# Second MLP of an attention-and-two-MLPs kernel: splits for the output product placed earlier, row tiles stored within it, last pass in halves

## The chip, the cores and the metric

The kernel runs on one core of one Trainium2 chip. The metric is the time of one execution on the device in microseconds (us); the kernel before takes 1617.16 us (median of three runs, 1616.46 to 1618.07). PE is the matrix engine, PEld its weight loads, DVE the vector engine, ACT the scalar engine, POOL the third elementwise engine, SP the engine that issues nearly all DMAs of this part.

## What is computed

A packed attention, a first MLP and a second MLP. Only the second MLP is touched:

```python
def _moe2_ref(x, w_in, w_out):          # x: 4608 x 512, w_in: 512 x 2048, w_out: 2048 x 512
    h = x @ w_in
    relu6 = np.clip(h + 3.0, 0.0, 6.0)
    g = h * relu6 / 6.0
    return (g @ w_out).astype(np.float32)
```

## The kernel before

Class `Second` computes the second MLP, transposed, so that tokens lie along the free dimension. It runs six passes ("pairs", n = 0 to 5) of 768 tokens, each two groups of N = 384. In each pair `hidden(n)` makes `x @ w_in` and the activation, and `project(n)` makes the output product. Both products are cut in 2 x 2 blocks and computed by seven block products instead of eight (numbers k = 1 to 7, with sums of blocks before and after). Each fp32 operand is split in a high part (an ACT cast, `split_hi`, L1136) and a low part (a DVE subtraction, `split_lo`, L1141), and each block product is three matmuls: high weights by high and by low data, low weights by high data (L1097 to L1099 in `hidden`, L1181 to L1183 in `project`). All matmuls are 128 x 384.

`hidden` has 56 steps (f, k): f = 0 to 7, seven products for each, 6 matmuls a step, in the order of `order_h`: the products of f overlap those of f + 1. After a step, `after(f, k)` queues the sums that read its PSUM bank: `h1` (ACT copy, then DVE L1067), `hu` (DVE L1058, later L1070) and `hv` (DVE L1061, L1062). A later product accumulates into a bank that such a sum still has to read, so PE waits for the sum. For each of the four blocks of f, ACT then computes a Relu (L1042) and DVE the gate (L1045), which writes the tile `g`. `soon(steps, fn)` delays a piece of work by some steps. For each odd f the two columns f - 1 and f of a g tile are complete; then `t1` (DVE L1116) and the two halves of the split of the first operand follow. These splits feed steps s = 0 to 3 of `project`, so four of them are made in `hidden`, one for each pair of f.

`project` has 28 steps, seven products (order 1, 5, 6, 3, 7, 2, 4) of four steps, 12 matmuls a step. Step s also queues the sums of step s + 4 and the split of step s + 3. There are four split buffers (`ro`). Step 0 of `project` is issued before the last two steps of `hidden`. The seven products end in the tiles `o1`, `ou`, `ov` and `oc`, each two blocks of 128 output columns for 384 tokens. `ou` is complete after step 15 and `ov` after step 19 and one add on POOL (L1169); these two hold the second 384 tokens of the pair. `oc` is complete after step 23 and `o1` after step 27, for the first 384.

`store` turns a 128-token tile back with four PE transposes into a PSUM bank, multiplies by 1/6 on ACT into `st` (three buffers) and issues one DMA of 128 rows, or, for tokens of the ninth and last block, two of 64 rows, on SP. The six stores of a pair wait in the list `out`; `hidden` of the next pair takes one every seven steps. The stores of the last pair run after its last product.

Weights come from DRAM in tiles `ws` of 512 KB (two DMAs, L962), six buffers, on SP: after each `project` step, and after every second `hidden` step, the next tile is requested into the buffer just used, so a tile is requested six tiles ahead. SP, ACT and DVE work strictly in the order in which the program issues.

Of the kernel before, what the change touches and what calls it, by code (L numbers as in the profile page):

```python
# [18 lines left out]
def tile_pack_attention_two_mlps(ctx: ExitStack, tc, q, k, v, p, w_in1, w_out1, w_in2, w_out2, out):  # L19
# [8 lines left out]
    nc = tc.nc  # L28
    B, H, S, D = q.shape
# [3 lines left out]
    P = 128  # L33
    T = 512
    NI = T // P
    TAIL = S - T
# [3 lines left out]
    KC = DM // P  # L40
# [26 lines left out]
    ident = const.tile([P, P], F32, name="ident")  # L67
# [16 lines left out]
    early, busy, other = [True], [True], [False]  # L84
# [571 lines left out]
    for j in range(2, B - 1):  # L656
        c, d = QPB * (j + 2), QPB * (j + 1)
# [266 lines left out]
    N = 384  # L924
    NPAIR = NBLK * T // (2 * N)
    ROW = {1: 0, 2: 1, 4: 2, 5: 3, 6: 4, 7: 5, 3: 6}
    ORDER_P = (1, 5, 6, 3, 7, 2, 4)
    FD = HF // 2
    WS = 6

    class Second:
# [94 lines left out]
        def hidden(self, n):  # L1026
            X, Y, Z, h1, hu, hv = {}, {}, {}, {}, {}, {}
            later = []

            def soon(steps, fn):  # L1030
                later.append([steps, fn])

            def run_later():
                for item in list(later):
                    item[0] -= 1
                    if item[0] <= 0:
                        later.remove(item)
                        item[1]()

            def act(f, part, h):  # L1040
                r = self.left.tile([P, N], F32, tag="hr", name="hr", bufs=4)
                nc.scalar.activation(out=r, in_=h, func=AF.Relu, bias=three)  # L1042

                def gate():
                    nc.vector.scalar_tensor_tensor(out=self.g[part, f // 2][:, f % 2], in0=r, scalar=6.0, in1=h, op0=ALU.min, op1=ALU.mult)  # L1045

                soon(1, gate)

            def small(tag):
                return self.left.tile([P, N], F32, tag=tag, name=tag, bufs=2)  # L1050

            def after(f, k):
                if k == 1:
                    h1[f] = small("h1")
                    nc.scalar.copy(out=h1[f], in_=X[f])
                elif k == 6:
                    hu[f] = small("hu")
                    nc.vector.tensor_add(out=hu[f], in0=h1[f], in1=Y[f])  # L1058
                elif k == 7:
                    hv[f] = small("hv")  # L1060
                    nc.vector.tensor_add(out=hv[f], in0=h1[f], in1=Y[f])  # L1061
                    nc.vector.tensor_add(out=hv[f], in0=hv[f], in1=Z[f])  # L1062
                    act(f, (1, 1), hv[f])
                elif k == 2:
                    act(f, (0, 0), X[f])
                elif k == 4:
                    nc.vector.tensor_add(out=h1[f], in0=h1[f], in1=Y[f])  # L1067
                    act(f, (1, 0), h1[f])
                elif k == 3:
                    nc.vector.tensor_add(out=hu[f], in0=hu[f], in1=Z[f])  # L1070
                    act(f, (0, 1), hu[f])
                    if f % 2:
                        soon(2, lambda: self.t1(f // 2))
                        soon(3, lambda: self.split_hi(f // 2))
                        soon(5, lambda: self.split_lo(f // 2))

            for fd in range(FD):
                for part in ((0, 0), (0, 1), (1, 0), (1, 1)):
                    self.g[part, fd] = self.left.tile([P, 2, N], F32, tag=f"g{part[0]}{part[1]}{fd}", name=f"g{part[0]}{part[1]}{fd}")
            seq = self.order_h()  # L1080
            xs = self.x
            for i, (f, k) in enumerate(seq):
                if i == len(seq) - 2:
                    next(self.projected)
                if i % 2 == 0:
                    w = self.weights()
                if k == 1:
                    X[f] = self.bank()[:, 0:N]
                elif k == 6:
                    Y[f] = self.bank()[:, 0:N]  # L1090
                elif k == 5:
                    Z[f] = self.bank()[:, 0:N]
                ps = {1: X, 2: X, 6: Y, 7: Y, 4: Y, 5: Z, 3: Z}[k][f]
                for c in range(2):
                    wh, wl = (w[:, i % 2, a + c * P:a + (c + 1) * P] for a in (0, 2 * P))
                    first, last = k in (1, 6, 5) and c == 0, k in (2, 4, 3) and c == 1
                    mm(ps, lhsT=wh, rhs=xs[k][:, 0, c], start=first, stop=False, skip_group_check=True)  # L1097
                    mm(ps, lhsT=wh, rhs=xs[k][:, 1, c], start=False, stop=False, skip_group_check=True)  # L1098
                    mm(ps, lhsT=wl, rhs=xs[k][:, 0, c], start=False, stop=last, skip_group_check=True)  # L1099
                if i % 2:  # L1100
                    self.load_w()
                run_later()
                after(f, k)
                if i % S7 == 5 and self.out:
                    self.out.pop(0)()
                if i == len(seq) // 2 and self.prep:
                    next(self.prep)
            while later:
                run_later()
            while self.out:  # L1110
                self.out.pop(0)()
# [36 lines left out]
        def project(self, n):  # L1148
            X, Y, Z = [], [], []
            o1, ou, ov, o5, oc = (self.left.tile([P, 2, N], F32, tag=tag, name=tag) for tag in ("o1", "ou", "ov", "o5", "oc"))  # L1150

            def after(k):
                for i in range(2):
# [17 lines left out]
            for s in range(FD * S7):  # L1171
                k, fd = ORDER_P[s // FD], s % FD
                w, ro = self.weights(), self.ro.pop(s)
                acc = {1: X, 2: X, 6: Y, 7: Y, 4: Y, 5: Z, 3: Z}[k]
                if not acc:
                    acc += [self.bank()[:, 0:N] for _ in range(2)]
                for f in range(2):
                    for i in range(2):
                        wh, wl = (w[:, f, a + i * P:a + (i + 1) * P] for a in (0, 2 * P))
                        first, last = k in (1, 6, 5) and fd == f == 0, k in (2, 4, 3) and fd == FD - 1 and f == 1  # L1180
                        mm(acc[i], lhsT=wh, rhs=ro[:, 0, f], start=first, stop=False, skip_group_check=True)  # L1181
                        mm(acc[i], lhsT=wh, rhs=ro[:, 1, f], start=False, stop=False, skip_group_check=True)  # L1182
                        mm(acc[i], lhsT=wl, rhs=ro[:, 0, f], start=False, stop=last, skip_group_check=True)  # L1183
                self.load_w()
                if s % FD == FD - 1:
                    after(k)
                self.sums(s + 4)
                if s + 3 >= FD:
                    self.split(s + 3)
                if self.prep and s and s // FD % 2 == 0:  # L1190
                    next(self.prep, None)
                yield
            if self.prep:
                for _ in self.prep:
                    pass
            for t in range(3):
                self.out.append(lambda t=t: self.store(2 * N * n + N + t * P, (ou, ov), t))
            for t in range(3):
                self.out.append(lambda t=t: self.store(2 * N * n + t * P, (oc, o1), t))

        def store(self, col, halves, t):

            ps = self.bank()
            for e in range(KC):
                nc.tensor.transpose(ps[:, e * P:(e + 1) * P], halves[e // 2][:, e % 2, t * P:(t + 1) * P], ident)
            o = self.left.tile([P, DM], F32, tag="st", name="st", bufs=3)
            nc.scalar.mul(out=o, in_=ps, mul=1.0 / 6.0)
            j, c = divmod(col, T)
            if j < B:
                i = c // P  # L1210
                nc.sync.dma_start(out=out[j * S:j * S + T, :].rearrange("(p i) e -> p i e", i=NI)[:, i, :], in_=o)
            else:
                rows = out.rearrange("(b s) e -> b s e", s=S)[:, T:S]
                for i in range(P // TAIL):
                    nc.sync.dma_start(out=rows[c // TAIL + i], in_=o[i * TAIL:(i + 1) * TAIL])

        def run(self):
            self.left = opened(ctx, "second_l", reuse_waits="tile")
# [168 lines left out]
    for j in range(NBLK):  # L1387
        ws = WINDOWS[j] if j < len(WINDOWS) else []
        order = []
        n = QPB * (j + 1) - 1  # L1390
# [13 lines left out]
        if j in mates:  # L1404
            for g in range(1, NG):
                fs = fuse_steps(j, g)
                lo, hi = [max(0, 18 * g * GF - 24) / (18 * NF) for g in (g - 1, g)]
                for i, fn in enumerate(fs):
                    plan.add(("m", j, g, i), lo + (hi - lo) * 0.7 * (i + 0.5) / len(fs), 6 if len(mates[j]) == 1 else 3, fn, bank=11)
        if j + 1 in mates:  # L1410
            lo = max(at_pp, (18 * 3 * GF - 24) / (18 * NF))
# [86 lines left out]
```

## Time and profile before

| | |
|---|---|
| median of three runs | 1617.16 us |
| span of the profiled execution | 1616.0 us |
| PE busy | 1546.7 us (96%) |
| DVE busy | 1036.1 us (64%) |
| ACT busy | 805.9 us (50%) |
| second MLP, first pair to the end | 876.4 to 1616.0 us |

The span runs from the first to the last instruction of one profiled execution. A busy PE is not PE at its best here: a matmul is shown as 0.34 us long while the next begins 0.17 us after it, so what a wait costs is read from the starts of the matmuls. In the rows further down, a bracket at a row's end is the idle time of the engine before it, and who ended it.

### The profile page before, as it was taken

How to read it: one execution, taken by the hardware profiler on the slowest of the kernel's cores; microseconds unless marked ns; L12 is line 12 of the kernel's file. 1: busy time of each engine (PE TensorE's matmuls, PEld its weight loads, DVE VectorE, ACT ScalarE, POOL GpSimd, SP SyncE). 2: the span in 40 equal slices, each digit the busy share in tenths (PEclk: the TensorE clock that was granted, in tenths of full speed). 3: DMA queues.
4: the chain of work that ended last, by engine and by line, in shares of the span. 5: the costliest groups of instructions: out<-in, count | busy, mean ns of one | idle time of the engine just before them, and what ended most of it. 6: DMA issues, size and time to landing. Idle time of an engine off the chain costs nothing.

```text
span 1616.0 us, 23717 instructions
## 1 busy us (share of the span) xinstructions
PE 1546.7 (96%) x8396; PEld 1333.6 (83%) x8396; DVE 1036.1 (64%) x1765; ACT 805.9 (50%) x1357; POOL 194.4 (12%) x172
## 2 busy tenths in 40 slices
PE   6898998899999999999999999999999999999997
PEld 3576765677777777778888999999999999999997
DVE  5776453765566465653443687687687687687674
ACT  4876544655556546554443353453453453453443
POOL 1432011111121111112231000000000000000000
PEclk9899999999999999999999999999999999999999
DMA  8998785896768776758597878978878988888875
GB/s 213 289 276 271 231 225 122 244 256 178 200 212 223 219 177 204 243 155 245 185 334 230 280 237 255 297 253 257 300 252 255 298 254 253 298 256 255 258 255 160
DMA packets 409750, 388.02 MB, mean 240 GB/s; under 512 B 156192, under 2 KB 282144, under 8 KB 409632
## 3 DMA queue, kind: packets, MB, share of 16 engines
q1 hardware_dynamic: 398256, 371.81, 76.7%
q10 hardware_dynamic: 11376, 14.68, 2.7%
q8 instruction: 68, 1.11, 0.3%
q14 instruction: 50, 0.41, 0.1%
HBM read 324.53 MB, written 61.87 MB: 239 GB/s over the span
## 4 chain that ended last, share of the span: by engine, by line
PE 61%; DVE 16%; ACT 11%; DMA 6%; issue 3%; SPq 2%; POOL 1%; ACTq 0%; DVEq 0%; POOLq 0%
PE b L1182 7%; PE b L1183 6%; PE b L1181 6%; PE acc L852 6%; PE acc L853 6%; PE acc L854 5%; ACT hr L1042 4%; DVE g L1045 3%; PE hps L829 3%; PE b L1097 3%; PE b L1099 3%; PE b L1098 3%; PE hps L831 3%; PE hps L830 3%; DVE ro L1141 1%
## 5 line engine op out<-in xcount | busy, mean ns | idle before, releaser
L1182 PE MATMUL b<-ro,ws 128*128 128x384 f32 x672 | 226.6, 337 | 6.3 <-DVE ro L1141 6.3
L1097 PE MATMUL b<-xc,ws 128*128 128x384 f32 x672 | 229.0, 341 | 3.3 <-DVE hv L1061 2.7
L1183 PE MATMUL b<-ro,ws 128*128 128x384 f32 x672 | 225.9, 336 | 0.0
L1181 PE MATMUL b<-ro,ws 128*128 128x384 f32 x672 | 225.9, 336 | 0.0
L1099 PE MATMUL b<-xc,ws 128*128 128x384 f32 x672 | 225.0, 335 | 0.0
L1098 PE MATMUL b<-xc,ws 128*128 128x384 f32 x672 | 224.7, 334 | 0.0
L845 DVE TENSOR_TENSOR gl<-hps,gh 128x512 fp32r<-128x512 f32 x144 | 99.1, 688 | 169.6 <-ACT gh L844 169.1
L1136 ACT CAST ro<-g 128x768 fp32r<-128x768 f32 x168 | 138.3, 835 | 101.9 <-DVE g L1130 36.5
L1141 DVE TENSOR_TENSOR ro<-g,ro 128x768 fp32r<-128x768 f32 x168 | 158.7, 953 | 8.9 <-ACT ro L1136 7.5
L837 ACT ACTIVATE hps<-hps 128x512 f32<-128x512 f32 x144 | 84.1, 584 | 110.0 <-PE hps L831 109.4
L1182 PEld LDWEIGHTS b<-ro,ws 128*128 128x128 f32 x672 | 126.4, 188 | 8.2 <-DVE ro L1141 8.2
L1097 PEld LDWEIGHTS b<-xc,ws 128*128 128x128 f32 x672 | 126.2, 188 | 7.7 <-DVE hv L1061 4.9
L1183 PEld LDWEIGHTS b<-ro,ws 128*128 128x128 f32 x672 | 126.4, 188 | 0.0
L1181 PEld LDWEIGHTS b<-ro,ws 128*128 128x128 f32 x672 | 126.4, 188 | 0.0
L1098 PEld LDWEIGHTS b<-xc,ws 128*128 128x128 f32 x672 | 126.3, 188 | 0.0
L1099 PEld LDWEIGHTS b<-xc,ws 128*128 128x128 f32 x672 | 126.2, 188 | 0.0
L852 PE MATMUL acc<-gh,wo 128*128 128x512 f32 x288 | 117.7, 409 | 0.0
L852 PE MATMUL acc<-gh,wr 128*128 128x512 f32 x288 | 117.7, 409 | 0.0
L853 PE MATMUL acc<-gl,wr 128*128 128x512 f32 x288 | 113.6, 394 | 0.1
L854 PE MATMUL acc<-gh,wr 128*128 128x512 f32 x288 | 113.4, 394 | 0.0
L853 PE MATMUL acc<-gl,wo 128*128 128x512 f32 x288 | 113.3, 393 | 0.0
L854 PE MATMUL acc<-gh,wo 128*128 128x512 f32 x288 | 113.1, 393 | 0.0
(261 smaller groups left out, 3002.2 us busy)
## 6 DMA issues: line engine op xcount, KB each, us to landing
ws<-w2in SPq DMA_DIRECT2D x336, 256.0 KB, 4.0
ws<-w2out SPq DMA_DIRECT2D x336, 256.0 KB, 3.6
wi<-w1i SPq DMA_DIRECT2D x80, 512.0 KB, 6.0
wo<-w1o SPq DMA_DIRECT2D x64, 512.0 KB, 5.5
x1d<-x SPq DMA_DIRECT2D x18, 512.0 KB, 5.7
w1i<-win SPq DMA_DIRECT2D x16, 512.0 KB, 7.7
praw<-in_moe_w_in_dram SPq DMA_DIRECT2D x32, 256.0 KB, 5.4
praw<-in_moe_w_out_dram SPq DMA_DIRECT2D x32, 256.0 KB, 4.7
```

The lines of the kernel that those rows point to most:

```text
L845: nc.vector.tensor_sub(out=gl, in0=g, in1=f32(gh))
L852: mm(acc[e], lhsT=w[:, 0, s], rhs=gh, start=first, stop=False)
L853: mm(acc[e], lhsT=w[:, 0, s], rhs=gl, start=False, stop=False)
L854: mm(acc[e], lhsT=w[:, 1, s], rhs=gh, start=False, stop=last)
L1097: mm(ps, lhsT=wh, rhs=xs[k][:, 0, c], start=first, stop=False, skip_group_check=True)
L1098: mm(ps, lhsT=wh, rhs=xs[k][:, 1, c], start=False, stop=False, skip_group_check=True)
L1099: mm(ps, lhsT=wl, rhs=xs[k][:, 0, c], start=False, stop=last, skip_group_check=True)
L1136: nc.scalar.copy(out=t[:, 0], in_=self.operand(s))
L1141: nc.vector.tensor_sub(out=t[:, 1], in0=self.operand(s), in1=f32(t[:, 0]))
L1181: mm(acc[i], lhsT=wh, rhs=ro[:, 0, f], start=first, stop=False, skip_group_check=True)
L1182: mm(acc[i], lhsT=wh, rhs=ro[:, 1, f], start=False, stop=False, skip_group_check=True)
L1183: mm(acc[i], lhsT=wl, rhs=ro[:, 0, f], start=False, stop=last, skip_group_check=True)
```

## The change

Three edits. In `hidden`, the split of the first operand is queued two and three steps after product 2 of an odd f (the product whose gate completes that operand) instead of three and five steps after product 3; `t1` stays where it was. In `project`, three of the six stores of a pair, those of `ou` and `ov`, are queued after steps 22, 23 and 24 of the product itself instead of in the next pair's `hidden`. In the last pair, the `oc` half of the other three tiles is stored after steps 25, 26 and 27, and only the `o1` half is left for the end; `store` can therefore do two transposes, half a multiplication and half a row tile.

```diff
@@ hidden, after(f, k)
                 elif k == 2:
                     act(f, (0, 0), X[f])
+                    if f % 2:
+                        soon(2, lambda: self.split_hi(f // 2))
+                        soon(3, lambda: self.split_lo(f // 2))
...
                     act(f, (0, 1), hu[f])
                     if f % 2:
                         soon(2, lambda: self.t1(f // 2))
-                        soon(3, lambda: self.split_hi(f // 2))
-                        soon(5, lambda: self.split_lo(f // 2))
@@ project
+            last_pair = n == NPAIR - 1
+            early = [lambda t=t: self.store(2 * N * n + N + t * P, {0: ou, 1: ov}, t) for t in range(3)]
+            if last_pair:
+                early += [lambda t=t: self.store(2 * N * n + t * P, {0: oc}, t) for t in range(3)]
...
+                if s >= FD * 5 + 2 and s - FD * 5 - 2 < len(early):
+                    early[s - FD * 5 - 2]()
                 yield
...
             for t in range(3):
-                self.out.append(lambda t=t: self.store(2 * N * n + N + t * P, (ou, ov), t))
-            for t in range(3):
-                self.out.append(lambda t=t: self.store(2 * N * n + t * P, (oc, o1), t))
+                if last_pair:
+                    self.out.append(lambda t=t: self.store(2 * N * n + t * P, {1: o1}, t))
+                else:
+                    self.out.append(lambda t=t: self.store(2 * N * n + t * P, {0: oc, 1: o1}, t))
@@ store
-            for e in range(KC):
-                nc.tensor.transpose(ps[:, e * P:(e + 1) * P], halves[e // 2][:, e % 2, t * P:(t + 1) * P], ident)
+            lo, hi = min(halves) * 2 * P, (max(halves) + 1) * 2 * P
+            for h, src in halves.items():
+                for e in range(2):
+                    nc.tensor.transpose(ps[:, (2 * h + e) * P:(2 * h + e + 1) * P], src[:, e, t * P:(t + 1) * P], ident)
             o = self.left.tile([P, DM], F32, tag="st", name="st", bufs=3)
-            nc.scalar.mul(out=o, in_=ps, mul=1.0 / 6.0)
+            nc.scalar.mul(out=o[:, lo:hi], in_=ps[:, lo:hi], mul=1.0 / 6.0)
```

The DMAs of `store` write the columns lo to hi likewise.

DVE in `hidden` of the second pair, from the `hu` sum of f = 6 on. g_9578 (before) and g_9602 (after) is the operand of step s = 2, which f = 4 and 5 fill. Before:

```order
L1058 TENSOR_TENSOR hu<-h_10071,b 128x384
L1067 TENSOR_TENSOR h_9982<-h_9982,b 128x384
L1045 SCALAR_TENSOR_TENSOR g_9580<-hr,h_9982 128x384
L1070 TENSOR_TENSOR hu<-hu,b 128x384
L1045 SCALAR_TENSOR_TENSOR g_9579<-hr,hu 128x384
L1061 TENSOR_TENSOR hv<-h_10071,b 128x384
L1062 TENSOR_TENSOR hv<-hv,b 128x384
L1116 TENSOR_TENSOR g_9579<-g_9579,g_9578 128x768
L1045 SCALAR_TENSOR_TENSOR g_9585<-hr,hv 128x384
L1045 SCALAR_TENSOR_TENSOR g_9582<-hr,b 128x384
L1058 TENSOR_TENSOR hu<-h_10155,b 128x384
L1141 TENSOR_TENSOR ro<-g_9578,ro 128x768
```

And after:

```order
L1058 TENSOR_TENSOR hu<-h_10079,b 128x384
L1070 TENSOR_TENSOR h_10001<-h_10001,b 128x384
L1142 TENSOR_TENSOR ro<-g_9602,ro 128x768
L1045 SCALAR_TENSOR_TENSOR g_9604<-hr,h_10001 128x384
L1073 TENSOR_TENSOR hu<-hu,b 128x384
L1045 SCALAR_TENSOR_TENSOR g_9603<-hr,hu 128x384
L1061 TENSOR_TENSOR hv<-h_10079,b 128x384
L1062 TENSOR_TENSOR hv<-hv,b 128x384
L1117 TENSOR_TENSOR g_9603<-g_9603,g_9602 128x768
L1045 SCALAR_TENSOR_TENSOR g_9609<-hr,hv 128x384
L1045 SCALAR_TENSOR_TENSOR g_9606<-hr,b 128x384
```

The low half of the split moves from behind the next `hu` sum to between the `h` sum and its gate; nothing else changes places.

DVE where `hidden` of the second pair ends and its `project` begins: the last sums and gates of f = 7 (g_9582 before, g_9606 after, is the operand of step s = 3; g_9571 and g_9595 that of step 4). Before:

```order
L1067 TENSOR_TENSOR h_10155<-h_10155,b 128x384
L1045 SCALAR_TENSOR_TENSOR g_9584<-hr,h_10155 128x384
L1070 TENSOR_TENSOR hu<-hu,b 128x384
L1045 SCALAR_TENSOR_TENSOR g_9583<-hr,hu 128x384
L1116 TENSOR_TENSOR g_9583<-g_9583,g_9582 128x768
L1141 TENSOR_TENSOR ro<-g_9582,ro 128x768
L1141 TENSOR_TENSOR ro<-g_9571,ro 128x768
```

And after:

```order
L1070 TENSOR_TENSOR h_10158<-h_10158,b 128x384
L1045 SCALAR_TENSOR_TENSOR g_9608<-hr,h_10158 128x384
L1073 TENSOR_TENSOR hu<-hu,b 128x384
L1142 TENSOR_TENSOR ro<-g_9606,ro 128x768
L1045 SCALAR_TENSOR_TENSOR g_9607<-hr,hu 128x384
L1117 TENSOR_TENSOR g_9607<-g_9607,g_9606 128x768
L1142 TENSOR_TENSOR ro<-g_9595,ro 128x768
```

The split for step 3 now stands ahead of the last gate and of `t1`.

ACT at the end of the last pair, from the split of step 24 on. Before:

```order
L1136 CAST ro<-g_14575 128x768
L1136 CAST ro<-g_14579 128x768
L1165 COPY oc<-b 128x384 x2
L1136 CAST ro<-g_14583 128x768
L1136 CAST ro<-g_14587 128x768
L1207 ACTIVATE st<-b 128x512 x6
```

And after:

```order
L1137 CAST ro<-g_14599 128x768
L1137 CAST ro<-g_14603 128x768
L1217 ACTIVATE st<-b 128x512
L1170 COPY oc<-b 128x384 x2
L1137 CAST ro<-g_14607 128x768
L1217 ACTIVATE st<-b 128x512
L1137 CAST ro<-g_14611 128x768
L1217 ACTIVATE st<-b 128x512
L1217 ACTIVATE st<-b 128x256 x6
```

Three whole tiles are multiplied within the product and six halves follow; the first three halves are `oc`, the last three `o1`.

## Rows read from the trace of the kernel before

**Rows 1.** Busy time in stretches: pair 0, 1, 5, and the end behind it.

```profile
core 0: us, PE busy (x) PEld busy (x) DVE busy (x) ACT busy (x) POOL busy (x), PEclk, DMA share, GB/s
876.35:996.82 120.47, 118.09 (x673) 116.26 (x672) 90.97 (x135) 52.54 (x82) 2.44 (x1) 1.00 0.81 259
996.82:1118.23 121.41, 120.03 (x697) 118.97 (x697) 91.63 (x136) 54.85 (x87) 2.40 (x1) 1.00 0.85 269
1482.41:1604.07 121.66, 119.99 (x697) 118.90 (x697) 82.20 (x125) 49.60 (x80) 2.40 (x1) 1.00 0.75 237
1604.07:1616.00 11.93, 2.78 (x25) 2.54 (x23) 0.75 (x2) 3.37 (x6) 0.00 (x0) 0.82 0.52 133
```

**Rows 2.** Waits from 890 us on: who waited for whom, us, times, longest.

```profile
PE b L1182 <- DVE ro L1141: 6.3, 6, 1.1
...
PE b L1097 <- DVE hv L1061: 2.7, 7, 0.6
...
PE b L1097 <- DVE hu L1058: 0.6, 2, 0.3
```

**Rows 3.** Timeline of PE, pair 1, steps 2 to 4 of project: start, length, line.

```profile
1062.83 0.34 PE L1181 MATMUL b<-ro,ws 128*128 128x384 f32 x1
...
1064.91 0.34 PE L1181 MATMUL b<-ro,ws 128*128 128x384 f32 x1
1066.28 0.44 PE L1182 MATMUL b<-ro,ws 128*128 128x384 f32 x1 [1.03 <-DVE ro L1141]
...
1068.32 0.34 PE L1181 MATMUL b<-ro,ws 128*128 128x384 f32 x1
```

**Rows 4.** Timeline of DVE: pair 0 (hv sums of f = 5, 6, 7), then pair 1.

```profile
920.64 0.55 DVE L1061 TENSOR_TENSOR hv<-h,b 128x384 f32<-128x384 f32 x1
...
927.77 0.55 DVE L1061 TENSOR_TENSOR hv<-h,b 128x384 f32<-128x384 f32 x1
...
936.51 0.55 DVE L1061 TENSOR_TENSOR hv<-h,b 128x384 f32<-128x384 f32 x1
...
1052.64 0.55 DVE L1045 SCALAR_TENSOR_TENSOR g<-hr,b 128x384 f32<-128x384 f32 x1 [0.98 <-ACT hr L1042]
...
1055.68 0.56 DVE L1045 SCALAR_TENSOR_TENSOR g<-hr,h 128x384 f32<-128x384 f32 x1 [0.68 <-ACT hr L1042]
...
1063.80 0.56 DVE L1045 SCALAR_TENSOR_TENSOR g<-hr,hu 128x384 f32<-128x384 f32 x1 [0.74 <-ACT hr L1042]
...
1065.27 1.82 DVE L1141 TENSOR_TENSOR ro<-g,ro 128x768 fp32r<-128x768 f32 x2
```

**Rows 5.** Timeline of ACT, pair 1, the split of step 2.

```profile
1051.29 0.83 ACT L1136 CAST ro<-g 128x768 fp32r<-128x768 f32 x1
```

**Rows 6.** Waits of SP's own queue, 876 to 1604 us.

```profile
SPq L1211 <- ACT st L1207: 46.6, 28, 3.5
```

**Rows 7.** The weight loads (line L962): time from issue to landing.

```profile
DMA to landing us min/median/max: 2.5/3.8/9.1
```

**Rows 8.** Timeline of POOL and PE, pair 1: the add into ov, project step 23.

```profile
1102.54 2.40 POOL L1169 TENSOR_TENSOR ov<-ov,o 128x768 f32<-128x768 f32 x1 [119.02 <-DVE ov L1163]
...
1107.84 0.34 PE L1181 MATMUL b<-ro,ws 128*128 128x384 f32 x1
```

**Rows 9.** Timeline of the end: PE, then ACT, then SP.

```profile
1604.07 0.38 PE L1205 MATMUL b<-ident,ou 128*128 128x128 f32 x2
1604.29 0.38 PE L1205 MATMUL b<-ident,ov 128*128 128x128 f32 x2
...
1604.70 1.58 ACT L1207 ACTIVATE st<-b 128x512 f32<-128x512 f32 x3 [6.81 <-PE b L1205]
...
1611.09 0.60 ACT L1207 ACTIVATE st<-b 128x512 f32<-128x512 f32 x1 [0.80 <-DMA out_dram<-st]
...
1605.33 3.76 SPq L1215 DMA_DIRECT2D out_dram<-st  x6
1609.18 1.48 SPq L1211 DMA_DIRECT2D out_dram<-st  x2
1611.71 1.11 SPq L1215 DMA_DIRECT2D out_dram<-st  x2
```

More of the change, by code (lines that the diff above doesn't have):

```diff
@@ L1210, in store @@
                 i = c // P
-                nc.sync.dma_start(out=out[j * S:j * S + T, :].rearrange("(p i) e -> p i e", i=NI)[:, i, :], in_=o)
+                nc.sync.dma_start(out=out[j * S:j * S + T, :].rearrange("(p i) e -> p i e", i=NI)[:, i, lo:hi], in_=o[:, lo:hi])
             else:
-                rows = out.rearrange("(b s) e -> b s e", s=S)[:, T:S]
+                rows = out.rearrange("(b s) e -> b s e", s=S)[:, T:S, lo:hi]
                 for i in range(P // TAIL):
-                    nc.sync.dma_start(out=rows[c // TAIL + i], in_=o[i * TAIL:(i + 1) * TAIL])
+                    nc.sync.dma_start(out=rows[c // TAIL + i], in_=o[i * TAIL:(i + 1) * TAIL, lo:hi])
         def run(self):
```

## Prediction

> **What bounds the kernel now.** I first read the busy time by pair, to see whether one engine sets the pace of the second MLP. PE is busy nearly the whole of each pair, at a granted clock of 1.00 throughout [rows 1]. But a matmul is shown twice as long as the distance to the next, so the busy share hides lost time. The distance is (1064.91 - 1062.83) / 12 = 0.173 us [rows 3], and a transpose takes 0.11, two in 0.22 [rows 9]. A pair has 672 matmuls, 116.5 us, and from pair 1 on 24 transposes, 2.6 us. So pair 1 should take 119.1 us and takes 121.4; pairs 2 to 4 are like it; pair 0, without stores, should take 116.5 and takes 120.5; pair 5 should take 119.1 and takes 121.7 [rows 1]. PE thus loses 4.0 + 4 x 2.3 + 2.6 = 15.8 us over the six pairs.
>
> The waits tell to whom. The longest are six waits of a low-part matmul for the DVE half of a split, one for each pair; then nine shorter ones in `hidden`, for `hv` and `hu` sums [rows 2]. The reader is to see that all of them are DVE being late, not DMA and not PSUM. The end is a separate stretch: 11.9 us behind the last matmul, in which ACT, SP and the DMAs write six row tiles one behind another [rows 1, 9].
>
> **Part 1, the wait at step 3.** In pair 1 step 3 runs from 1064.91 to 1068.32, 3.41 us instead of 2.08, since its second matmul waits until 1066.28 for the low half that DVE began at 1065.27 [rows 3, 4]. That is 1.33 us with the slower restart, of which 1.03 is shown as idle; six pairs, 8.0 us (6.3 by idle time alone). DVE has this split at the end of a queue: `hu` sum, a round trip to ACT, gate at 1063.80, `t1`, then the split. In the new order the split stands directly behind the `hu` sum, in the 0.74 us in which DVE waits for the Relu [rows 4]. Counted back from 1065.27, the gate and `t1` (together 1.47 us) now come behind it, so its low half starts at the latest at about 63.1 and is done by 64.05 (+1000), against a need at 65.08, the second matmul of step 3. If the wait in `hidden` below goes too, PE comes 0.9 us earlier, but DVE then gains more than that. What is late next is the split for step 4. It now ends where the one for step 3 ended or earlier, 1066.1, and step 4 would ask for it at 68.49 - 1.33 = 67.2: 1.1 us to spare. I take the whole 8.0.
>
> **Part 2, the same split in `hidden`.** The other 15.8 - 8.0 = 7.8 us are lost in `hidden`, and the cause is again the place of the split. In pair 0, where no stores slow PE, the `hv` sums of f = 5, 6 and 7 start at 920.64, 927.77 and 936.51 [rows 4]. An f without late work takes DVE 7.13 us; one with `t1` and the split takes 8.74. PE needs 7 x 6 x 0.173 = 7.28 us per f. So DVE falls back 1.46 us in every second f, recovers 0.15 in the others, and when the reserve of three steps (3.1 us) is gone PE waits. The 1.6 us come from `t1`, from the split (0.87 each, back to back) and from the ACT half of the split, 0.83 us, which stands ahead of a Relu and leaves DVE idle for 0.98 [rows 4, 5]. In the new order the ACT half comes while ACT is waiting for the `h` sum, and the DVE half fills the 0.68 us of the next round trip, as `t1` already fills another of 0.74. Each then costs 0.13 to 0.19 us beyond its cover: such an f takes 7.13 + 0.3 = 7.45 at most, on average 7.29 against PE's 7.28. DVE no longer falls back, and the reserve of 3.1 us stays. Not all of the 7.8 us is waiting; the first matmul behind a store starts a little slower, and that stays. Idle time alone is 2.7 + 0.6 = 3.3 us [rows 2]; I take 7.0, nearer to what the pair lengths give. Cover that goes: three stores of each pair leave `hidden`, 12 transposes x 0.11 = 1.3 us in which DVE used to catch up. Pair 0 shows the worst of that: it has none and loses 4.0 instead of 2.3.
>
> **Part 3, three stores inside the product.** In pairs 0 to 4 the transposes only move: 0. Each thing moved has its cover. The transposes after step 22 need the POOL add. It ends at 1104.94, and step 23, before which they now stand, starts at 1107.84: 2.9 us to spare [rows 8]. The PSUM banks come round after eight, and the nearest one asked for, that of the third store, is read by the `oc` copy a step earlier. ACT has 0.6 us more per step, in which it was idle about half. SP gets a store's DMA between two weight loads; it waits for ACT there, as the stores in `hidden` did for up to 3.5 us [rows 6]. Behind it stand loads that are asked for five `project` steps, 10.4 us, ahead of their use and land after 3.8 us, at most 9.1 [rows 7].
>
> **Part 4, the last pair.** Three whole stores and the first two `oc` halves come ahead of the last matmul's end: 16 transposes x 0.11 = 1.8 us added on PE. What this buys lies behind the last matmul. Before, from the first transpose at 1604.07 to the end is 11.9 us: ten DMA issues on SP, and three stores that wait for one of the three `st` buffers [rows 9]. After, count from the same point as zero. The third `oc` half: two transposes, ACT starts at 0.4 (before 0.63, behind four), half a multiplication 0.35 (an estimate between half and all of the 0.60 of a whole one), two DMA issues on SP at 0.63 each, done at 2.0. Its buffer is free 2.0 later (before, the sixth issue ended at 1609.09 and the multiplication waiting for it began at 1611.09), at 4.0. The last `o1` half needs just this buffer: ACT 0.35, two issues 1.11, and then the 3.2 us that before lie between the last issue's end, 1612.82, and the end of the span. That is 8.7 us, 3.2 less. The other two `o1` halves fit on ACT and SP in between. Net: 3.2 - 1.8 = 1.4 us gained, with 0 and 2.5 as ends, as the half DMAs land no faster or well faster and the multiplication costs its whole 0.60 or half.
>
> **Sum.** 1616.0 - 8.0 - 7.0 - 1.4 = 1599.6 us of span. The median of the runs is 1.2 above the span, so 1600.8.
>
> **Rivals.** (a) *The late sums in `hidden` stay late.* The same DVE work is done in the same stretch, and PE loses its stores there, so DVE is no better covered than now. For it: the average of 7.29 us against 7.28 has no margin. Against it: a lag has to add up to 3 us first. Only part 1 and 4 then count: 1600.8 + 7.0 = 1607.8. (b) *The change does little:* part 1 is won, but with three stores fewer all pairs behave like pair 0 and lose its 4.0 - 1.3 = 2.7 us in `hidden` instead of 1.0, 5 x 1.7 = 8.5 more: 1607.8 + 8.5 = 1616.3. For it: pair 0 itself; against it: pair 0 has the old order of DVE. (c) *A piece of the wait moves to the last gate.* The low half now stands ahead of the last gate and `t1`; if ACT's half is late, the split for step 4 is late by one operation, 0.87 us, in each pair: 5.2 us, 1606.0. Against it: the 1.1 us to spare. (d) *The loads stand behind the stores, and it gets slower.* Three stores in a row now sit in SP's queue in `project`, each followed by weight loads. If each holds the queue for the 3.5 us that the longest such wait takes now [rows 6] and the three add up, the loads behind are 10.5 us late; they have 10.4 - 3.8 = 6.6 to give, so PE would starve for 3.9 us in each pair: 6 x 3.9 = 23, about 1624. It decides once the three delays sum to more than 6.6 us; it is slower than before by the bound below from 1600.8 + 19.6 on, 9.9 us of delay per pair. Against it: the load behind a store must wait for the end of its own step in any case, 2.1 us later, and ACT's queue is not full. Here a rule of the Trainium skill speaks against the change: its page "Perfetto Trace Analysis", section "DMA Optimizations", advises one DMA-issuing engine for inputs and another for outputs, which the change goes further from. By that rule case (d) would be the expected one. The trace agrees that stores do hold the loads' queue, 46.6 us in 28 waits [rows 6], but shows no wait of PE for a weight tile among its waits [rows 2].
>
> **How the numbers follow.** Forecast 0.75, (a) 0.12, (b) 0.04, (c) 0.06, (d) 0.03. The range takes in the bounds of the forecast, down to 1598.9, rounded to 1598.0, with the whole 15.8 us and the better tail, and up over (c) to the idle times alone, 1616.0 - 6.3 - 3.3 - 1.4 + 1.2 = 1606.2, rounded to 1607.0; (a), (b) and (d), 0.19, are left out. Within 0.2% (3.2 us, about what a measurement of this kernel can tell from no change) lies (b) alone, 0.04; (d) is slower, 0.03; the rest, 0.93, is faster.
>
> **What would show it.** Right: pairs 1 to 4 take 119.1 to 119.5 us, pair 0 about 117.8 (three stores more), step 3 lasts 2.1 us, no PE wait for the split, for `hv` or for `hu` in the list, and 8 to 9.5 us behind the last matmul with the last multiplication waiting for a DMA. Part 2 is wrong if waits for `hv` or `hu` stay; part 3 if a transpose waits for the POOL add, or a matmul for a weight load near steps 24 to 27 or early in `hidden`; part 4 if the tail is over 10 us. The whole would be wrong if DVE were not what PE waits for, but only the last of several that end together.

## The result

The changed kernel takes 1599.9 us (median of four runs, 1596.7 to 1602.4) against 1616.8 us before (1615.1 to 1618.1): a ratio of 0.9897, 95% interval 0.9884 to 0.9910. The prediction was 1600.8 us, in a range of 1598 to 1607. The profiled execution has a span of 1594.9 us and is the shortest of the four.

The second MLP itself, from the first matmul of pair 0 to the end of the span, took 739.7 us before (876.35 to 1616.0) and takes 722.4 now (872.57 to 1594.9): 17.3 us less, where the sum said 16.4. The other 3.8 us by which the two profiled spans differ lie ahead of it, in code that is the same in both kernels. So the experiments below are compared by the length of the second MLP in the trace, which does not contain that part.

Busy time by pair in the changed kernel, the same stretches as in [rows 1] (pair 0, 1, 5, and behind the last matmul):

```profile
core 0: us, PE busy (x) PEld busy (x) DVE busy (x) ACT busy (x) POOL busy (x), PEclk, DMA share, GB/s
872.57:990.47 117.90, 117.90 (x686) 117.80 (x685) 91.18 (x135) 54.38 (x85) 2.45 (x1) 1.00 0.84 270
990.47:1109.77 119.30, 119.30 (x698) 119.09 (x698) 91.94 (x136) 55.28 (x87) 2.40 (x1) 1.00 0.85 274
1467.64:1587.43 119.79, 119.79 (x702) 119.48 (x702) 82.51 (x125) 50.95 (x82) 2.40 (x1) 1.00 0.77 244
1587.43:1594.90 7.47, 1.38 (x9) 0.81 (x7) 0.75 (x2) 1.43 (x4) 0.00 (x0) 0.81 0.27 71
```

PE is now busy through the whole of each pair, and the pairs last what their matmuls and transposes need: 117.9 and 119.3, against 120.5 and 121.4 before. The stretch behind the last matmul is 7.5 us instead of 11.9.

Of PE's waits from 872 us on, one is left, at the very end: the transposes of the last product wait 0.2 us for its sum. The columns are those of [rows 2].

```profile
PE b L1215 <- DVE o L1172: 0.2, 1, 0.2
```

Step 3 of the product in pair 1, which lasted 3.41 us in [rows 3], starts with the first of these two matmuls; the second is the first of step 4:

```profile
1056.40 0.34 PE L1186 MATMUL b<-ro,ws 128*128 128x384 f32 x1
...
1058.48 0.34 PE L1186 MATMUL b<-ro,ws 128*128 128x384 f32 x1
```

It takes 2.08 us, as every other step does.

### The profile page after: what moved, and what is told of

Its sections match the earlier page's. It is cut to its first block, busy times and chain, and to the rows that moved or that the text cites. A ratio compares the mean times of both kernels' runs of the same rounds, so it can differ in the third digit from the quotient of the medians.

```text
span 1594.9 us, 23740 instructions
## 1 busy us (share of the span) xinstructions
PE 1540.4 (97%) x8396; PEld 1334.8 (84%) x8396; DVE 1038.1 (65%) x1765; ACT 809.4 (51%) x1360; POOL 195.0 (12%) x172
## 3 DMA queue, kind: packets, MB, share of 16 engines
q8 instruction: 68, 1.11, 0.3%
## 4 chain that ended last, share of the span: by engine, by line
PE 78%; DVE 6%; ACT 6%; DMA 5%; SPq 2%; issue 2%; POOL 1%; ACTq 0%; DVEq 0%; POOLq 0%
PE b L1098 7%; PE b L1100 7%; PE b L1187 7%; PE b L1188 7%; PE b L1186 7%; PE b L1099 7%; PE acc L852 6%; PE acc L853 6%; PE acc L854 6%; PE hps L829 3%; PE hps L831 3%; PE hps L830 3%; PE abank L495 1%; PE b L1215 1%; DVE fused L624 1%
## 5 line engine op out<-in xcount | busy, mean ns | idle before, releaser
L1142 DVE TENSOR_TENSOR ro<-g,ro 128x768 fp32r<-128x768 f32 x168 | 159.4, 953 | 12.8 <-ACT ro L1137 12.1
```

What stands on the lines that cost most here:

```text
L1142: nc.vector.tensor_sub(out=t[:, 1], in0=self.operand(s), in1=f32(t[:, 0]))
```

## Experiments

Lengths in us. "Step 3" is the step in which PE used to wait for the last split; "hidden" is the time that PE lost above the length of its matmuls and transposes in the `hidden` steps and step 0, counting only steps that lost more than 0.11. Every line is one profiled execution; where two of these kernels are alike in pairs 1 to 4, the lengths agree within 0.1 (119.25 to 119.33 in five of them). A kernel for which the text gives no time of the whole was executed once.

| kernel | second MLP | pair 0 | pairs 1 to 4 | pair 5 | tail | step 3, each | hidden, sum |
|---|---|---|---|---|---|---|---|
| before | 739.7 | 120.5 | 121.4 | 121.7 | 11.9 | 3.4 | 6.3 |
| changed | 722.4 | 117.9 | 119.3 | 119.8 | 7.5 | 2.08 | 0 |
| splits alone | 724.8 | 116.5 | 119.3 | 119.3 | 11.9 | 2.08 | 0 |
| stores and halves alone | 743.8 | 121.8 | 122.7 | 123.5 | 7.5 | 3.4 | 12.3 |
| last split alone | 731.4 | 119.1 | 120.1 | 120.1 | 11.9 | 2.08 | 6.2 |
| first three splits alone | 727.6 | 117.0 | 119.7 | 119.7 | 11.9 | 2.55 | 0 |
| ACT half of the splits alone | 729.2 | 118.2 | 119.8 | 119.8 | 12.0 | 3.4, then 2.6 | 0.4 |
| changed, whole tiles at the end | 721.7 | 117.9 | 119.3 | 119.3 | 7.3 | 2.08 | 0 |
| changed, six `st` buffers | 721.9 | 117.9 | 119.3 | 119.8 | 7.0 | 2.08 | 0 |
| ... and ACT issues two DMAs | 721.9 | 117.9 | 119.3 | 119.8 | 7.0 | 2.08 | 0 |
| changed, two more DVE operations | 748.2 | 122.7 | 123.4 to 123.7 | 123.9 | 7.5 | 2.08 | 19.0 |
| changed, one more DVE operation | 724.8 | 118.8 | 119.5 to 119.7 | 120.1 | 7.5 | 2.08 | 1.4 |
| changed, five weight buffers | 726.6 | 118.4 | 119.8 to 120.9 | 119.8 | 7.5 | 2.08 | 3.8 |

**The splits alone.** The two hunks in `after(f, k)` on the kernel before, everything else as it was.

> Only the splits move; all stores stay where the kernel before has them. The length read is the second MLP, from the first matmul of its first pair to the end of the span: 739.6 us before, 722.3 in the changed kernel. Theory (the place of the split made all the waits): no PE wait for a split, for hv or hu is left, pair 0 takes 116.6 us, pairs 1 to 4 take 119.3, the tail stays 11.9: second MLP 724.5, time 1602. Rival (moving the stores was part of it): some waits for hv or hu stay, 728 or more.

Measured: second MLP 724.8, no wait of PE at all in it. The time is 1604.1 us (1599.8 to 1609.6), a ratio of 0.9915 to the kernel before on the same chip (0.9887 to 0.9942). PE in the whole stretch from the first matmul of pair 0 to the end of the last product:

```profile
core 0: us, PE busy (x) PEld busy (x) DVE busy (x) ACT busy (x) POOL busy (x), PEclk, DMA share, GB/s
875.12:1587.97 712.85, 712.85 (x4153) 711.88 (x4152) 542.39 (x799) 323.35 (x510) 14.18 (x6) 1.00 0.84 267
```

All the waits came from the place of the splits; of the 17.3 us the splits give 14.9.

**The stores and halves alone.** The changed `project` and `store`, with the splits in their old places.

> Only the stores move and the last pair is halved; the splits stay in their old places. Theory (stores in the hidden stretch were cover for DVE): the wait at step 3 stays 1.3 us in each pair, the waits for hv and hu in pairs 1 to 5 grow from 1.0 towards the 2.7 of pair 0, I expect about 1.9, and the tail gains 2.5 net: second MLP 739.6 + 4.5 - 2.5 = 741.6, time 1619. Rival (the stores cover nothing): waits as before, second MLP 737.

The time is 1624.8 us (median of ten runs, 1619.5 to 1627.0), a ratio of 1.0036 (1.0023 to 1.0049): this half of the change by itself makes the kernel slower. Its waits of PE, columns as in [rows 2]:

```profile
PE b L1186 <- DVE ro L1141: 6.2, 6, 1.1
PE b L1097 <- DVE hv L1061: 4.5, 12, 0.6
PE b L1097 <- DVE hu L1058: 2.1, 7, 0.3
```

The wait for the last split is what it was, but there are 12 waits for `hv` instead of 7 and 7 for `hu` instead of 2. Every pair now loses in `hidden` nearly what only pair 0 lost (2.5 us): 1.9 us in pairs 1 to 4, as expected, but up from 0.7, not from the 1.0 that the expectation started at. The stores had been cover for DVE. The expectation was 2.2 us too low on the whole: the waits come to 5.9 us more than before instead of 4.5, and the remaining 0.8 is in steps that lost too little to be counted.

**The last split alone, and the first three alone.**

```diff
 # last split alone: in the k == 2 branch
+                    if f == HF - 1:
+                        soon(2, lambda: self.split_hi(f // 2))
+                        soon(3, lambda: self.split_lo(f // 2))
 # and in the k == 3 branch
-                        soon(3, lambda: self.split_hi(f // 2))
-                        soon(5, lambda: self.split_lo(f // 2))
+                    if f % 2 and f < HF - 1:
+                        soon(3, lambda: self.split_hi(f // 2))
+                        soon(5, lambda: self.split_lo(f // 2))
```

The other kernel has the two conditions exchanged.

> Of the four splits made in the hidden stretch only the last one (f = 7, for step 3) moves. Theory: step 3 loses its 1.33 us in each pair, 8.0 in all, the waits for hv and hu stay as before: second MLP 731.6. Rival (the last split is late only because DVE has fallen back earlier): less than half of the 8.0 goes, 736 or more.

> Only the first three splits (f = 1, 3, 5) move, the last stays behind t1. Theory: the waits for hv and hu go (7 us); and since DVE no longer arrives late at the last steps, the wait at step 3 shrinks from 1.33 to about 0.4 us: second MLP 739.6 - 7 - 5.6 = 727. Rival (the two waits are independent): the wait at step 3 stays 1.33, second MLP 732.6.

The last split alone, waits of PE:

```profile
PE b L1101 <- DVE hv L1061: 2.4, 7, 0.4
PE b L1101 <- DVE hu L1058: 0.6, 2, 0.3
```

and the first three alone:

```profile
PE b L1186 <- DVE ro L1145: 1.1, 6, 0.2
```

Each of the two takes away its own wait: the `hv` and `hu` waits remain in the one, the wait for the split in the other. But the second remainder is small. With DVE no longer behind, step 3 loses 0.47 us instead of 1.33, although its split still stands behind `t1`. The gains are 8.3 and 12.1 us, together 20.4, and both at once give 14.9: most of the wait at step 3 had two causes, and either cure is enough for it.

**Only the ACT half early.**

```diff
 # k == 2 branch
+                    if f % 2:
+                        soon(2, lambda: self.split_hi(f // 2))
 # k == 3 branch
-                        soon(3, lambda: self.split_hi(f // 2))
                         soon(5, lambda: self.split_lo(f // 2))
```

> Only the ACT half of the four splits moves to the early place; the DVE half stays in the old one. Theory (the ACT half standing ahead of a Relu cost DVE 0.98 - 0.30 of idle time): an f with late work takes DVE 8.74 - 0.68 = 8.06 us instead of 8.74, it falls back 0.78 and recovers 0.15, so the reserve of three steps lasts through a pair and the waits for hv and hu go or nearly go; the wait at step 3 shrinks to about 0.4: second MLP 727 to 729. Rival (it is the DVE half that counts): more than half of the waits stays, 733 or more.

```profile
PE b L1183 <- DVE ro L1142: 2.3, 6, 1.0
```

DVE's `hv` sums of f = 2 and 3 in pair 0:

```profile
897.52 0.55 DVE L1061 TENSOR_TENSOR hv<-h,b 128x384 f32<-128x384 f32 x1
...
905.52 0.55 DVE L1061 TENSOR_TENSOR hv<-h,b 128x384 f32<-128x384 f32 x1
```

The f with late work takes DVE 8.00 us now (`hv` sum to `hv` sum), where 8.06 was expected and 8.74 was before, and no wait for `hv` or `hu` is long enough for the list of waits. This half of the move alone gives 10.5 of the 14.9 us. So a good part of what the old place cost was not DVE's own operation but ACT's, which stood ahead of a Relu that DVE then waited for. In pair 0, which has no stores, the reserve (the time from the end of a sum on DVE to the matmul that writes its bank again) does run out: 0.4 us lost in `hidden` and a full wait at step 3. That puts the sum at 729.2, just above the expected band.

**Whole tiles, six buffers, a second queue at the end.** Three variants of the changed kernel: `last_pair = False`; `bufs=6` for `st`; and `bufs=6` with the two DMAs of the third `oc` half issued by `nc.scalar` instead of `nc.sync`.

> The changed kernel, but the last pair is treated like the others: ou and ov stored within the product, three whole tiles of oc and o1 behind it, no halves. Theory (in the changed kernel the last half waits 1.7 us for one of three st buffers, which whole tiles would not): PE ends 0.5 us earlier and the tail is no longer than the 7.5 us of the changed kernel, second MLP 721.5 instead of 722.3. Rival (halves pay, as half the work is left behind the last matmul): 723.5 or more.

> The changed kernel with six st buffers instead of three. Theory: the last multiplication no longer waits 1.7 us for a DMA; then SP's queue of issues is what is late, and the tail goes from 7.5 to about 6.6 us: second MLP 721.4. Rival (the end is set by the issues on SP and the landing alone): unchanged, 722.3.

> The changed kernel with six st buffers, and the two DMAs of the third oc half issued by ACT instead of SP. Theory (with six buffers the tail of 7.0 us is SP's queue of six DMA issues, 0.5 to 0.6 us each): two issues fewer ahead of the last ones, tail 6.1, second MLP 721.0. Rival (landing and the closing instructions set the end): tail stays 7.0.

The end of the changed kernel, with PE, ACT and SP as in [rows 9]:

```profile
1587.43 0.38 PE L1215 MATMUL b<-ident,oc 128*128 128x128 f32 x2
...
1587.89 0.39 ACT L1217 ACTIVATE st<-b 128x256 f32<-128x256 f32 x1 [1.93 <-PE b L1215]
...
1590.99 0.38 ACT L1217 ACTIVATE st<-b 128x256 f32<-128x256 f32 x1 [1.69 <-DMA out_dram<-st]
...
1588.30 1.11 SPq L1225 DMA_DIRECT2D out_dram<-st  x2
1589.54 1.01 SPq L1221 DMA_DIRECT2D out_dram<-st  x2
1591.40 1.11 SPq L1225 DMA_DIRECT2D out_dram<-st  x2
```

and with whole tiles, SP alone:

```profile
1595.17 0.83 SPq L1221 DMA_DIRECT2D out_dram<-st  x2
1596.15 1.11 SPq L1225 DMA_DIRECT2D out_dram<-st  x2
```

Whole tiles leave four DMA issues behind the last matmul instead of six and wait for no buffer; the tail is 7.3 us, and PE has four transposes fewer ahead of it. The last issue then ends 3.9 us behind the last product instead of 5.1, but the span ends 3.3 us after that issue, where with half rows it is 2.4. On balance the halves gain nothing: 721.7 without them, 722.4 with them. Six buffers shorten the tail by 0.5, half of what was expected. The second queue gives nothing more, since the two issues now take time on ACT, ahead of the multiplications that the last DMAs need; these start 3.4 us behind the last product, with six buffers alone 3.5:

```profile
1596.78 1.21 ACTq L1225 DMA_DIRECT2D out_dram<-st  x2
1598.04 0.94 ACT L1217 ACTIVATE st<-b 128x256 f32<-128x256 f32 x3 [1.28 <-PE b L1215]
```

None of the three differs from the changed kernel by more than its runs spread: medians 1600.8 (whole tiles, 1597.8 to 1603.3), 1600.0 (six buffers, 1599.1 to 1601.7) and 1602.3 (second queue, 1598.5 to 1605.2).

**More work for DVE.** In the changed kernel, one or two subtractions of 128 x 768, whose result nobody uses, are queued behind each of the four low halves in `hidden`.

```diff
                         soon(3, lambda: self.split_lo(f // 2))
+                        soon(3, lambda: self.spare(f // 2))
...
+        def spare(self, s):
+            t = self.left.tile([P, 2, N], F32, tag="spare", name="spare")
+            for _ in range(2):
+                nc.vector.tensor_sub(out=t, in0=self.operand(s), in1=self.operand(s))
```

> The changed kernel with two more DVE subtractions of 128x768 (0.87 us each, back to back) behind the low half of each of the four splits; their result is used by nobody. Theory (DVE breaks even with PE, 7.28 us per f, with a reserve of about 2.5 to 3.1 us): three such loads before the last hv sum add 5.2 us, the reserve and the three stores take 2.8 to 4.1 of it, so PE waits for hv or hu 1 to 2.4 us in each pair, some 8 in all: second MLP 731. Rival (DVE, 77% busy in a pair, has room): no waits, 722.3.

```profile
PE b L1099 <- DVE hv L1061: 15.4, 12, 1.4
PE b L1193 <- DVE ro L1143: 3.8, 6, 0.9
```

The kind of wait was right and the size far off: 25.8 us instead of 9. An f with this load takes DVE 9.17 us, so three of them put it some 5.4 us behind, net, at the last `hv` sum of a pair, as assumed. But the reserve is smaller. In the changed kernel the `hv` sum of f = 5 in pair 0, and the first matmul of the product that waits for its end:

```profile
914.07 0.55 DVE L1061 TENSOR_TENSOR hv<-h,b 128x384 f32<-128x384 f32 x1
...
916.26 0.33 PE L1098 MATMUL b<-xc,ws 128*128 128x384 f32 x1
```

DVE is done at 914.62, 1.6 us ahead of PE, not 2.5 to 3.1: even without extra work it is done a step and a half behind the product whose sum it makes. At the last `hv` sum of the pair, f = 7, the distance is the same, 1.65 us; in the kernel before it was 0.05 there. Besides, the fourth load makes step 4 of the product wait 0.9 us for its split in each pair, where it had been taken for covered, and the three stores take only 0.5 off (pairs 1 to 4 lose 3.1 us in `hidden`, pair 0 loses 3.6). With one operation instead of two:

> The changed kernel with one more DVE subtraction of 128x768 behind the low half of each of the four splits. Theory (DVE breaks even with PE and its reserve is only about 1.65 us, not 3.1): three loads of 0.94 add 2.6 us net of what is recovered, so PE waits about 1.0 us in pair 0 and 0.6 in the others, second MLP 726. Rival (what an added DVE operation costs is in proportion, half of the 25.9 us that two cost): 735. Rival (the reserve is 3.1): 722.4.

Measured 724.8, with one counted wait of PE, in pair 0, where `hidden` loses 0.8 us:

```profile
PE b L1099 <- DVE hv L1061: 0.4, 1, 0.4
```

Half the load costs not half of 25.8 but 2.4 us, so it is a threshold, and the reserve of about 1.6 us describes pair 0. The other pairs lose only 0.1 each in the counted steps (0.2 to 0.4 in their whole length) where 0.6 was expected: behind the third store, at f = 2, their `hv` sum ends 1.5 us ahead of its product, in pair 0 only 0.8.

**One weight buffer less.** `WS = 5` instead of 6 in the changed kernel.

> The changed kernel with five weight buffers instead of six: each weight tile is requested 2.08 us later. Theory (by the trace of the changed kernel the tile of step 40 of the hidden stretch, behind the load of the next pair's x, lands only 0.4 to 1.4 us before its use in pairs 0 to 4; elsewhere 6 us are to spare): PE waits 0.7 to 1.7 us for weights once in each of these five pairs, 6 us in all, second MLP 728. Rival (the landing times shift with the requests, or the loads have more room than that): 722.3 to 723.

```profile
PE b L1098 <- DMA ws<-w2in: 2.9, 5, 1.3
```

Five waits, one for each pair that loads the next pair's `x`, and 4.2 us on the whole, where 6 was expected. Each request came 2.08 us later and cost 0.4 to 1.5 us at that place. So with six buffers the loads have an estimated 0.6 to 1.7 us to spare there, and are next to the edge at that one place.

## Why the prediction was right, step by step

The sum said 16.4 us for the second MLP and 17.3 came: the stages below are where the forecast is tested. That the median of the runs lies within 0.9 us of the forecast is in part luck, since the four runs spread over 5.7 us and one of them, at 1596.7, lies below the stated range.

**What bounds the kernel.** Right: PE, with DVE as the only one that it waited for. Taking away DVE's lateness leaves no wait.

**Part 1, step 3.** Forecast 8.0 us; 6 x 1.33 went, and no other wait took its place. The part treated this wait as a matter of one split's place. The two kernels with part of the splits show a second cause behind it, DVE's lag in `hidden`, which alone accounts for 0.86 of the 1.33.

**Part 2, hidden.** Forecast 7.0 us. With the splits alone the pairs add up to 712.85 us against 727.72, 14.9 less, so 6.9 go to this part. The mechanism shows in DVE's rows of the changed kernel, pair 0, to be read against [rows 4]:

```profile
918.26 0.96 DVE L1142 TENSOR_TENSOR ro<-g,ro 128x768 fp32r<-128x768 f32 x1
919.14 0.55 DVE L1045 SCALAR_TENSOR_TENSOR g<-hr,h 128x384 f32<-128x384 f32 x1
...
921.38 0.55 DVE L1061 TENSOR_TENSOR hv<-h,b 128x384 f32<-128x384 f32 x1
...
928.63 0.55 DVE L1061 TENSOR_TENSOR hv<-h,b 128x384 f32<-128x384 f32 x1
```

The gate behind the split has no idle time before it any more; the 0.68 us of the round trip is filled. From `hv` to `hv` DVE takes 7.31 us with the split in it (914.07 to 921.38) and 7.25 with `t1` (921.38 to 928.63), on average 7.28, where 7.29 was the estimate and PE needs 7.28. The average was right and its parts were not: the prediction had split and `t1` in the same f, 7.45 at most, and 7.13 for the other, while the early split falls in the f before that of `t1`. Wrong in this part was also the size of the reserve, 3.1 us: measured 1.6 at that sum. It was not needed for the time, only for the first experiment with added work, which was 17 us off, some 10 of them in `hidden` for that reason, 5.5 by the wait at step 4.

**Part 3, stores in the product.** Forecast 0, and right: in pairs 1 to 4 the kernel with the splits alone and the changed one both take 119.3 us. Cover for the loads was enough; what SP's own queue waited for in the changed kernel, and the landing of its weight loads, as in [rows 6, 7]:

```profile
SPq L1221 <- ACT st L1217: 27.3, 30, 2.0
...
SPq L1225 <- ACT st L1217: 4.9, 3, 2.3
...
DMA to landing us min/median/max: 2.6/3.8/9.5
```

Stores hold the loads' queue for 32 us in all and 2.3 at most, less than the 46.6 and 3.5 before. Stores and loads share SP's queue in both kernels, and no run with six weight buffers shows PE waiting for a weight tile. The Trainium skill's page "Perfetto Trace Analysis", section "DMA Optimizations", advises to part input from output queues and gives no price for not doing so. That advice named no loss that this kernel has.

**Part 4, the end.** Forecast a tail of 8.7 us; it is 7.5, shorter than the 8 to 9.5 that the prediction named as its sign. PE's extra transposes cost 1.9 us (1.4 more in pair 0, 0.5 in pair 5), where 1.8 was forecast, so the net gain is about 2.5 instead of 1.4 (2.4 by the second MLPs of the splits alone and of the changed kernel), at the upper end given. The order of events was right, down to the last half waiting for a buffer. Mis-sized were two landings taken over from whole tiles: the buffer came free 1.6 us after its second issue ended (1589.41 to 1590.99), not 2.0, and the span ended 2.4 us after the last issue (1592.51 to 1594.9), not 3.2. With whole tiles in the changed kernel the span ends 3.3 us after the last issue, so the old figure held for whole rows. What the part did not see is that the halves are not needed; the gain is from the three whole tiles that leave earlier.

**Rivals.** (b), that pairs without stores fall back to what pair 0 lost, is real as a mechanism: alone, the stores do just this and the kernel gets slower. It does not happen here, since the moved splits end the lag that the stores covered. (a) and (c) did not happen. (d) did not either: the queue is held less than before.

## What to carry to other kernels

When an engine that works strictly in order alternates with another one, its idle time of each round trip can be the place for late work. Here the low half of the split cost DVE about 0.17 us there (the gate starts 1.40 us after the start of the `h` sum instead of 1.23); in the old place it cost 0.87, and its ACT half another 0.7 us of DVE's idle time. Before moving work away from the bounding engine's path, see whether it was giving a slower engine time to catch up; one half of a change can be a loss by itself and free beside the other. A reserve is read from the trace (end of the producer to start of the consumer), not from the number of steps between the two in the program.

## What was not expected

Over the thirteen kernels profiled here, the first matmul of the second MLP came between 872.6 and 881.3 us, although the program ahead of it is the same in all but the one with five weight buffers, which loads a weight tile less ahead. That is half of the gain under study, and it shifts whole spans: the three variants of the end have second MLPs of 721.7 to 721.9 us and spans of 1597.4 to 1602.9. What causes it no run here tested. And the two issues of 64-row DMAs that were moved to ACT kept that engine's queue for 1.21 us, as long as on SP (1.11), so a second issuing engine was no gain where that engine has work of its own.
